# Attention backward for one query: half of V's gradient stored by GpSimd in pieces, in eight of 32 pairs

## Chip, cores and metric

One core of a Trainium2 chip. The metric is the device time of one execution in microseconds; lower is better. The core has the engines PE (TensorE), DVE (VectorE), ACT (ScalarE), POOL (GpSimd) and SP (SyncE), and sixteen DMA engines which all DMA queues share.

## What is computed

Attention of one query per head over 8192 keys, forward and backward, in bfloat16; 2 batches of 32 heads give 64 heads of 128 dimensions.

```python
B, H, Sq, Sk, D = 2, 32, 1, 8192, 128
def _fwd_reference(q, k, v):
    scale = q.shape[-1] ** -0.5
    scores = jnp.einsum("bhqd,bhkd->bhqk", q, k) * scale
    p = _softmax(scores, axis=-1)
    return jnp.einsum("bhqk,bhkd->bhqd", p, v)

_out, _vjp = jax.vjp(_f, q, k, v)
return (_out, *_vjp(grad_out))        # out, dq, dk, dv
```

K and V are read once (268 MB), their gradients written once (268 MB). For a single query the gradients of K and V are outer products: of the score gradients with q, and of the softmax weights with the output's gradient.

## The kernel before

**Tiles.** Heads go in 32 pairs. A pair's K, or V, is a buffer of 128 partitions by 128 tiles of 128 numbers: 4 MB, 32 KB in a partition; head 0 fills partitions 0 to 63, head 1 the others. The buffers stand in a ring of six (`ring`), three pairs of K and V. V's gradient is written over V in its own buffer and K's over K; then the buffer is stored and loaded again for the pair three further on (K of pair g+3 goes where V of pair g was, V where K was).

**Stages.** A pair goes through 16 stages `j` of its own, in which K (0 to 7) and V (8 to 15) are turned by TensorE, 16 tiles a stage (`transposes`, L119, copied out of PSUM by ACT at L126 and four times a pair by DVE at L124), and multiplied with the query or the output's gradient one stage later (`products`, L136). What is left of the pair runs in stages 16 to 24, beside stages 0 to 8 of the next pair. `manual_schedule` keeps the order in which the code issues things; each engine runs its list in that order.

**Gradients.** The softmax weights are there after stage 11. From stage 12 on, TensorE forms the weighted sums (`weighted_rows`, L247), and DVE writes V's gradient chunk by chunk (`outer`, L275, 16 tiles of 128 x 2048 numbers a chunk), by these tables:

```python
OUT_V = {12: (0,), 13: (1, 2), 14: (3,), 15: (4, 5), 16: (6,), 17: (7,)}
OUT_K = {19: (0, 1), 20: (2,), 21: (3, 4), 22: (5,), 23: (6, 7)}
STORE = {18: 0, 24: 1}
```

Between them DVE computes `deltas` (L218, in the next pair's stage 0) and `weights_k` (L231 to L241, in its stage 1), which K's gradient needs. TensorE's `sums` (L187) of the second kind needs `deltas`. In stage 24 `combine` (L264) ends the pair's part on TensorE.

**DMA.** SP's queue issues all loads (`load`, L108), ACT's all stores (`store`, L283). At stage 18 the whole of V's gradient is stored by one DMA of 4 MB, and the load of K for the pair three further on is put behind it; at stage 24 the same is done with K's gradient and V's load. A load waits for the store that empties its buffer. The last pair's gradients go out in quarters of 1 MB. Two small loads of 16 KB (`nat`) at the start bring q and the output's gradient, and two small stores at the end write the output and q's gradient. GpSimd sets up constants at the start (its two `wz` memsets at L295) and then does nothing.

Of the kernel before, what the change touches and what calls it, by code (L numbers as in the profile page):

```python
# [11 lines left out]
BF16 = mybir.dt.bfloat16  # L12
# [2 lines left out]
CH = 16  # L15
HC = CH // 2
RING = 6


@with_exitstack  # L20
def kernel(
# [11 lines left out]
    nc = tc.nc  # L33
    B, H, Sq, D = q.shape
    Sk = k.shape[2]
    P = nc.NUM_PARTITIONS
# [4 lines left out]
    NT = 2 * Sk // P  # L41
    NCH = NT // CH
# [5 lines left out]
    const = ctx.enter_context(tc.tile_pool(name="const", bufs=1))  # L48
# [18 lines left out]
    q_rows = q.rearrange("b h s d -> (b h s) d")  # L67
# [4 lines left out]
    def by_pairs(x):  # L72
        rows = x.rearrange("b h s d -> (b h s) d")
        return rows.rearrange("(g p n) d -> g p n d", p=P, n=NT)

    k_v, v_v, dk_v, dv_v = (by_pairs(x) for x in (k, v, out_2, out_3))
# [8 lines left out]

    ring = [kvp.tile([P, NT, D], BF16, name=f"ring{i}") for i in range(RING)]
    acc = ps_one.tile([P, 4 * D], F32, name="acc", tag="acc")
# [12 lines left out]
    pairs = [Pair() for _ in range(NP)]  # L100
# [6 lines left out]
    def load(g, w):  # L107
        nc.sync.dma_start(out=pairs[g].kv[w][:], in_=(k_v, v_v)[w][g])  # L108
# [4 lines left out]
    def transposes(g, j, u):  # L113
        x = pairs[g]
        w, c = divmod(j, NCH)
        tp = ps_tp.tile([P, HC, P], F32, name="tp", tag="tp")
        for i in range(HC):
            n = c * CH + u * HC + i
            nc.tensor.matmul(  # L119
                tp[:, i, :], lhsT=x.kv[w][:, n, :], rhs=ident_bf[:], start=True, stop=True  # L120
            )
        ev = evp.tile([P, HC, P], BF16, name="ev", tag="ev")
        if (j, u) in ((8, 0), (9, 0), (10, 0), (11, 0)):
            nc.vector.tensor_copy(out=ev[:], in_=tp[:])  # L124
        else:
            nc.scalar.copy(out=ev[:], in_=tp[:])  # L126
        x.ev[j, u] = ev

    def products(g, j, u):
        x = pairs[g]  # L130
        w, c = divmod(j, NCH)
        ev = x.ev.pop((j, u))
        cols = (qT_all, doT_all)[w][:, 2 * g : 2 * g + 2]
        for i in range(HC):
            n = c * CH + u * HC + i
            nc.tensor.matmul(  # L136
                scores(w)[:, :, n], lhsT=ev[:, i, :], rhs=cols, start=True, stop=True
            )

    def spread_row(g, w):  # L140
        pb = misc[:, (2 + w) * D : (3 + w) * D]
        for s, hs in enumerate(halves):
            nc.tensor.matmul(  # L143
                pb[hs],
                lhsT=ident_bf[0:BH, 2 * g + s : 2 * g + s + 1].to_broadcast([BH, HP]),
                rhs=nat[:, 1 - w, :],
                start=True,
                stop=True,
            )
        x = pairs[g]  # L150
        x.row = rowp.tile([P, D], BF16, name="row", tag="row")
        nc.scalar.copy(out=x.row[:], in_=pb)  # L152
# [6 lines left out]
    def all_max(x):  # L159
        mT = sm[0:1, 2 * NT : 2 * NT + P]  # L160
        nc.tensor.transpose(mT, x.mp[:], ident_f[:])
        x.gm = work.tile([1, 2], F32, name="gm", tag="gm")
        nc.vector.reduce_max(out=x.gm[:], in_=mT.rearrange("o (s p) -> o s p", s=2), axis=AX.X)
# [21 lines left out]
    def sums(x, w):  # L185
        x.lsum = (dp if w else sm)[:, 2 * NT + P + 8 : 2 * NT + P + 9]
        nc.tensor.matmul(x.lsum, lhsT=block[:], rhs=x.ld[:, w : w + 1], start=True, stop=True)  # L187
# [55 lines left out]
    def weighted_rows(x, w, c):  # L243
        rows = x.kv[1 - w]
        for g in range(4):
            n = c * CH + 4 * g
            nc.tensor.matmul(  # L247
                acc[32 * g : 32 * g + 16, :],
                lhsT=wz[w][:, n // 4, :],
                rhs=rows[:, n : n + 4, :].rearrange("p n d -> p (n d)"),  # L250
                start=(w == 0 and c == 0),
                stop=(w == 1 and c == NCH - 1),
                tile_position=(0, 32 * g),
            )
# [5 lines left out]
    def combine(g):  # L260
        x = pairs[g]
        c = misc[:, 0:4]
        for j in range(4):
            nc.tensor.matmul(  # L264
                c, lhsT=x.accsb[:, j * D : (j + 1) * D], rhs=pick[:, j],
                start=(j == 0), stop=(j == 3),
            )
        nc.vector.tensor_copy(  # L268
            out=colsT[:, :, 2 * g : 2 * g + 2], in_=c.rearrange("p (w s) -> p w s", w=2)
        )  # L270

    def outer(x, w, c):
        n = c * CH
        row = x.row[:].rearrange("p (d t) -> p d t", t=2)
        nc.vector.tensor_tensor(  # L275
            out=x.kv[1 - w][:, n : n + CH, :].rearrange("p n (d t) -> p n d t", t=2),
            in0=row.unsqueeze(1).to_broadcast([P, CH, D // 2, 2]),
            in1=x.w2[w][:, n : n + CH, :].unsqueeze(2).to_broadcast([P, CH, D // 2, 2]),
            op=ALU.mult,
        )  # L280

    def store(g, w, a=0, b=NT):
        nc.scalar.dma_start(  # L283
            out=(dv_v, dk_v)[w][g][:, a:b, :], in_=pairs[g].kv[1 - w][:, a:b, :]
        )

    def outer_and_store(g, w, c):
        outer(pairs[g], w, c)
        if g == NP - 1 and c % 2:
            store(g, w, (c - 1) * CH, (c + 1) * CH)  # L290

    for i, src in enumerate((q_rows, do_rows)):
        nc.scalar.dma_start(out=nat[:, i, :], in_=src)
    for t in wz:
# [12 lines left out]
    STORE = {18: 0, 24: 1}  # L307

    with tc.manual_schedule():
        for g in range(RING // 2):  # L310
            load(g, 0)
            load(g, 1)
        for h in range(NP + 1):
            y = pairs[h] if h < NP else None
            x = pairs[h - 1] if h else None
            for j in range(NS):
                at = [(z, zg, s) for z, zg, s in ((x, h - 1, j + NS), (y, h, j)) if z]
                for u in range(2):
                    if y:
                        transposes(h, j, u)  # L320
                    if y and j:
                        products(h, j - 1, u)
                    elif x and j == 0:
                        products(h - 1, NS - 1, u)
                    if u == 0:
                        if y and j == 8:
                            spread_row(h, 0)
                        if x and j == 2:
                            spread_row(h - 1, 1)
                        if x and j == 8:  # L330
                            combine(h - 1)
                    else:
                        if y and j == 9:
                            all_max(y)
                        if y and j == 10:
                            exps(y)
                        if y and j == 11:
                            sums(y, 0)
                        if x and j == 1:
                            sums(x, 1)  # L340
                    if u == 1:
                        for z, zg, s in at:
                            for w, when in ((0, ACC_V), (1, ACC_K)):
                                for c in when.get(s, ()):
                                    weighted_rows(z, w, c)
                if y and j == 8:
                    row_max(y)
                if y and j == 11:
                    weights_v(y)
                if x and j == 0:  # L350
                    deltas(x)
                if x and j == 1:
                    weights_k(x)
                for z, zg, s in at:
                    if s in STORE and zg < NP - 1:
                        store(zg, STORE[s])
                        if zg + 3 < NP:
                            load(zg + 3, STORE[s])
                    for w, when in ((0, OUT_V), (1, OUT_K)):
                        for c in when.get(s, ()):  # L360
                            outer_and_store(zg, w, c)
                if x and j == 6:
                    acc_to_sbuf(x)
        for w, dst in enumerate((o_rows, dq_rows)):
            tps = ps_tp.tile([BH, P], BF16, name="tps", tag="tp")
            nc.tensor.transpose(tps[:], colsT[:, w, :], ident_bf[:])
            rows = evp.tile([BH, D], BF16, name=f"rows{w}", tag="ev")
            nc.scalar.copy(out=rows[:], in_=tps[:])
            nc.scalar.dma_start(out=dst, in_=rows[:])


# [28 lines left out]
```

## Time and profile before

| | |
|---|---|
| times of three runs | 1300.5 us median (1298.71 to 1301.36) |
| profiled execution | 1301.66 us, of it 1299.9 us span |
| mean granted TensorE clock | 0.85 |
| busy: PE, DVE, ACT, POOL | 1093.5, 930.0, 906.3, 2.0 us |
| DMA | 539.64 MB, 415 GB/s over the span |
| DMA queues of SP and ACT | 48.8% and 49.0% of sixteen engines' span |
| instruction fetch (two queues) | 2.69 MB, 0.7% |
| chain that ended last | DMA 63%, PE 24%, ACT 7%, DVE 3% |
| a load of 4 MB, from issue to landing | 27.6 to 27.8 us (median) |
| a store of 4 MB | 45.9 us (median) |

The span goes from the first instruction to the last. "Issue to landing" counts from the issuing instruction to the last of sixteen marks, one from each DMA engine that has done its share; a wait for a DMA ends with the sixteenth. A transfer spreads over the partitions, so each engine has a fixed share of the rows. A line such as `A <- B` in the waits says that A sat idle until B was done. Queue letters (SPq, ACTq) are an engine's issuing side.

### The profile page before, as it was taken

Reading aid. Unit: us, or ns where it says so; the run is one execution under the profiler, and the core shown is the slowest. Engines: PE = TensorE matmul, PEld = TensorE weight load, DVE = VectorE, ACT = ScalarE, POOL = GpSimd, SP = SyncE. Lnnn points to the kernel's source line nnn. Section 1 sums busy time; section 2 is a strip of 40 time slices with the busy share of each in tenths; the row PEclk is TensorE's granted clock in tenths of the full one; section 3 lists DMA queues with packets and bytes.
Section 4 is the critical chain, followed back from the end, with each engine's and each line's share of the span. In section 5 each row is a group of like instructions: output and inputs, shape, how many; then the busy total and the mean of one; then the engine's idle time right before and its main releaser. Section 6 shows DMA issues by size and latency. Waiting matters only on the chain.

```text
span 1299.9 us, 42160 instructions
## 1 busy us (share of the span) xinstructions
PE 1093.5 (84%) x19044; PEld 936.6 (72%) x19044; DVE 930.0 (72%) x1355; ACT 906.3 (70%) x1091; POOL 2.0 (0%) x10
## 2 busy tenths in 40 slices
PE   4999899988888889888888887898888988889883
PEld 3777787776777778777677776677677877778771
DVE  0888788767867677767786676776677666776775
ACT  4887778767866678757686576876578666786761
POOL 0000000000000000000000000000000000000000
PEclk9999989889988788868898688988788777887876
DMA  9999999999999999999999999999999999999986
GB/s 404 417 425 424 429 427 432 427 430 430 429 429 427 427 426 420 427 430 403 426 429 427 429 400 429 432 423 423 414 393 420 416 405 410 410 421 419 404 348 268
DMA packets 19796, 539.64 MB, mean 415 GB/s; under 512 B 2464, under 2 KB 2464, under 8 KB 2464
## 3 DMA queue, kind: packets, MB, share of 16 engines
q10 hardware_dynamic: 10400, 268.51, 49.0%
q1 hardware_dynamic: 9216, 268.44, 48.8%
q8 instruction: 149, 2.44, 0.7%
q14 instruction: 31, 0.25, 0.0%
HBM read 268.47 MB, written 268.47 MB: 413 GB/s over the span
## 4 chain that ended last, share of the span: by engine, by line
DMA 63%; PE 24%; ACT 7%; DVE 3%; issue 2%; ACTq 0%; SPq 0%; DVEq 0%
DMA ring<-in_v_dram 43%; DMA out_dram<-ring 19%; PE tp L119 15%; ACT ev L126 5%; PE misc L264 3%; PE dp L136 2%; PE acc L247 1%; DVE ring L275 1%; DMA nat<-in_grad_out_dram 1%; PE sm L136 1%; DVE ev L124 1%; PE sm L167 1%; ACT E_f L176 1%; ACT row L152 1%; PE sm L187 0%
## 5 line engine op out<-in xcount | busy, mean ns | idle before, releaser
L126 ACT CAST ev<-tp 128x1024 bf16<-128x1024 f32 x896 | 865.4, 1020 | 287.0 <-PE tp L119 273.4
L119 PE MATMUL tp<-ident_bf,ring 128*128 128x128 bf16 x8192 | 721.9, 240 | 148.7 <-DMA ring<-in_v_dram 73.8
L119 PEld LDWEIGHTS <-ring 128*128 128x128 bf16 x8192 | 581.3, 108 | 286.7 <-issue 189.6
L136 PEld LDWEIGHTS <-ev 128*128 128x128 bf16 x8192 | 338.3, 100 | 7.3 <-issue 5.7
L275 DVE TENSOR_TENSOR ring<-row,dS 128x2048 bf16<-128x2048 bf16 x256 | 298.9, 1220 | 41.7 <-PE acc L247 39.9
L275 DVE TENSOR_TENSOR ring<-row,P 128x2048 bf16<-128x2048 bf16 x256 | 300.2, 1221 | 36.8 <-PE acc L247 35.8
L124 DVE CAST ev<-tp 128x1024 bf16<-128x1024 f32 x128 | 156.7, 1225 | 135.1 <-PE tp L119 131.6
L136 PE MATMUL dp<-doT_all,ev 128*128 128x2 bf16 x4096 | 185.7, 167 | 2.2 <-issue 1.4
L136 PE MATMUL sm<-qT_all,ev 128*128 128x2 bf16 x4096 | 178.9, 165 | 3.8 <-issue 3.7
L247 PE MATMUL acc<-ring,wz 128*16 128x512 bf16 x2048 | 167.8, 396 | 3.2 <-DVE wz L191 2.3
L152 ACT CAST row<-misc 128x128 bf16<-128x128 f32 x64 | 18.1, 282 | 81.5 <-PE misc L143 74.8
L264 PE MATMUL misc<-pick,accsb 128*128 128x4 f32 x256 | 52.0, 326 | 17.5 <-ACT row L152 11.2
L264 PEld LDWEIGHTS misc<-pick,accsb 128*128 128x128 f32 x256 | 49.2, 286 | 23.2 <-ACT row L152 16.0
L247 PEld LDWEIGHTS <-wz 128*16 128x16 bf16 x2048 | 31.2, 86 | 11.0 <-issue 2.7
L218 DVE CUSTOM_DVE_ANT_0 dSu<-E_f,dp 64x128 f32<-64x128 f32 x64 | 18.3, 285 | 28.5 <-PE dp L136 28.0
L157 DVE TENSOR_REDUCE mp<-sm 64x1 f32<-64x128 f32 x64 | 18.5, 289 | 21.9 <-PE sm L136 21.2
L268 DVE CAST colsT<-misc 128x4 bf16<-128x4 f32 x32 | 5.1, 161 | 31.8 <-PE misc L264 31.8
L176 ACT ACTIVATE E_f<-sm,negm 64x128 f32<-64x128 f32 x64 | 23.2, 363 | 1.7
L236 DVE SCALAR_TENSOR_TENSOR dSu<-dp,negdelta,E_f 64x128 f32<-64x128 f32 x64 | 22.4, 350 | 2.2
L258 DVE COPY accsb<-acc 128x512 f32<-128x512 f32 x32 | 22.1, 692 | 2.0 <-PE acc L247 1.0
L191 DVE TENSOR_SCALAR wz<-dSu,rl 64x128 bf16<-64x128 f32 x64 | 18.1, 283 | 2.1
L191 DVE TENSOR_SCALAR wz<-E_f,rl 64x128 bf16<-64x128 f32 x64 | 18.1, 283 | 1.7
(42 smaller groups left out, 197.6 us busy)
## 6 DMA issues: line engine op xcount, KB each, us to landing
out_dram<-ring ACTq DMA_DIRECT2D x62, 4096.0 KB, 45.9
ring<-in_k_dram SPq DMA_DIRECT2D x32, 4096.0 KB, 27.6
ring<-in_v_dram SPq DMA_DIRECT2D x32, 4096.0 KB, 27.8
out_dram<-ring ACTq DMA_DIRECT2D x8, 1024.0 KB, 11.3
out_dram<-rows ACTq DMA_DIRECT2D x2, 16.0 KB, 9.7
nat<-in_q_dram ACTq DMA_DIRECT2D x1, 16.0 KB, 11.0
nat<-in_grad_out_dram ACTq DMA_DIRECT2D x1, 16.0 KB, 15.4
```

The lines of the kernel that those rows point to most:

```text
L119: nc.tensor.matmul(tp[:, i, :], lhsT=x.kv[w][:, n, :], rhs=ident_bf[:], start=True, stop=True)
L124: nc.vector.tensor_copy(out=ev[:], in_=tp[:])
L126: nc.scalar.copy(out=ev[:], in_=tp[:])
L136: nc.tensor.matmul(scores(w)[:, :, n], lhsT=ev[:, i, :], rhs=cols, start=True, stop=True)
L152: nc.scalar.copy(out=x.row[:], in_=pb)
L176: nc.scalar.activation(out=x.E[hs], in_=scores(0)[hs, s, :], func=ACT.Exp, bias=negm[hs], scale=scale, accum_out=x.ld[hs, 0:1],)
L191: nc.vector.tensor_scalar(out=wz[w][hs, :, 8 * w + 4 * s : 8 * w + 4 * s + 4], in0=src[hs].rearrange("p (m j) -> p m j", j=4), scalar1=s1[ ...
L236: nc.vector.scalar_tensor_tensor(out=x.dSu[hs], in0=scores(1)[hs, s, :], scalar=negdelta[hs], in1=x.E[hs], op0=ALU.add, op1=ALU.mult,)
L247: nc.tensor.matmul(acc[32 * g : 32 * g + 16, :], lhsT=wz[w][:, n // 4, :], rhs=rows[:, n : n + 4, :].rearrange("p n d -> p (n d)"), start= ...
L258: nc.vector.tensor_copy(out=x.accsb[:], in_=acc[:])
L264: nc.tensor.matmul(c, lhsT=x.accsb[:, j * D : (j + 1) * D], rhs=pick[:, j], start=(j == 0), stop=(j == 3),)
L275: nc.vector.tensor_tensor(out=x.kv[1 - w][:, n : n + CH, :].rearrange("p n (d t) -> p n d t", t=2), in0=row.unsqueeze(1).to_broadcast([P, ...
```

## The change

In pairs 1, 5, 9, ..., 29 (`RELIEF`, eight of them) the first half of V's gradient (tiles 0 to 63, 16 KB in a partition, 2 MB) is no longer part of ACT's store. As soon as DVE's chunk 3 has been issued (stage 14), GpSimd stores it by 24 DMAs, each of some rows (partitions) four apart. The pieces are laid out so that each group of rows goes to the DMA engines that move it in a full store, except the rows 16 to 19 and 48 to 51, the fifth engine's: these go out in four pieces of two rows (`fifth`) by way of eight other engines. For this the change counts on a place that goes round the sixteen engines with every GpSimd DMA, and moves that place on by small loads of 3 to 14 rows of 8 bytes from q into a spare tile (`turn`), eleven in an event, one at the start and one at the end. ACT's store at stage 18 sends the second half alone. K's load three pairs on now waits for both.

```diff
+RELIEF = range(1, 32, 4)
...
+    spare = const.tile([P // 8, 48], BF16)
+    turns = []
+
+    def turn(n):
+        i = 4 * (len(turns) % 12)
+        turns.append(n)
+        two = lambda t: t.rearrange("p (a b) -> p a b", a=2)
+        nc.gpsimd.dma_start(out=two(spare[0:n, i : i + 4]), in_=two(q_rows[0:n, 0:4]))
+
+    def store_by_fifteen(g):
+        dst, src = (t[:, 0 : NT // 2, :] for t in (dv_v[g], pairs[g].kv[1]))
+
+        def rows(lo, n, step=4, size=8192):
+            own = slice(lo, lo + step * (n - 1) + 1, step)
+            nc.gpsimd.dma_start(out=dst[own], in_=src[own], max_dma_last_dim=size)
+
+        def fifth(r):
+            rows(16 + r, 2, step=32)
+
+        for r in range(4):
+            if r == 1:
+                fifth(r)
+                turn(14)
+            rows(52 + r, 11)
+            rows(r, 4, size=16384)
+            if r == 0:
+                fifth(r)
+                turn(3)
+            elif r == 3:
+                turn(10)
+                fifth(r)
+                turn(9)
+            else:
+                turn(5)
+            rows(20 + r, 3)
+            if r == 2:
+                fifth(r)
+                turn(14)
+            rows(96 + r, 8)
+            rows(32 + r, 4, size=16384)
+            turn(5)
...
     def outer_and_store(g, w, c):
         outer(pairs[g], w, c)
+        if g in RELIEF and w == 0 and c == NCH // 2 - 1:
+            store_by_fifteen(g)
         if g == NP - 1 and c % 2:
             store(g, w, (c - 1) * CH, (c + 1) * CH)
...
+    turn(5)
     for i, src in enumerate((q_rows, do_rows)):
         nc.scalar.dma_start(out=nat[:, i, :], in_=src)
...
-                        store(zg, STORE[s])
+                        store(zg, STORE[s], NT // 2 if zg in RELIEF and not STORE[s] else 0)
...
             nc.scalar.dma_start(out=dst, in_=rows[:])
+        turn(11)
```

Every piece of 8 KB or 16 KB in a row is a packet or two on its engine; a full row of before is one packet of 32 KB. GpSimd's DMAs report to eight semaphores in turn, so each waits for the one eight before it.

## The prediction

> **What bounds the kernel now.** I read the page's slices first, then the windows by stage, the waits of SP's queue, the chain, and last DVE's timeline around the place of the edit.
>
> The slices say that the DMA engines never rest before the last 50 us, and that their rate falls late in the run:
>
> ```profile
> DMA  9999999999999999999999999999999999999986
> GB/s 404 417 425 424 429 427 432 427 430 430 429 429 427 427 426 420 427 430 403 426 429 427 429 400 429 432 423 423 414 393 420 416 405 410 410 421 419 404 348 268
> ```
>
> The windows put numbers on it (time, busy time of PE, PEld, DVE, ACT and POOL, then granted clock, DMA share, GB/s):
>
> ```profile
> 206.00:241.00 35.00, 31.45 (x595) 26.72 (x595) 29.24 (x43) 28.42 (x35) 0.00 (x0) 0.95 1.00 429
> 120.00:560.00 440.00, 379.95 (x6789) 325.28 (x6788) 332.25 (x479) 323.86 (x389) 0.00 (x0) 0.88 1.00 427
> 960.00:1240.00 280.00, 245.10 (x4073) 212.11 (x4071) 199.16 (x291) 194.49 (x234) 0.00 (x0) 0.80 1.00 413
> 1292.00:1298.00 6.00, 0.00 (x0) 0.00 (x0) 0.00 (x0) 0.00 (x0) 0.00 (x0) 0.50 0.06 26
> ```
>
> Share 0.06 is one engine of sixteen: one engine works alone for the last 6 us. It is slower all along. In the trace's packet records a 32 KB packet takes 1.213 us on most engines, and on one chain of back-to-back packets (330 to 362 us) mostly 1.22 to 1.34 us. The landing marks of the stores show it too: its mark trails the last but one by 2.3 us at 231 us, 14 at 574, 25 at 979, and then no more, since the others have run out of stores to work ahead on. From there the kernel goes at this engine's pace, 413 GB/s for 427. So what the change is after is there.
>
> SP's waits and the chain say how loads hang on stores, and how fast the compute engines are when data is there:
>
> ```profile
> SPq L108 <- DMA out_dram<-ring: 1174.6, 58, 50.7
> ```
>
> ```profile
> 65.70 1.06 PE misc L264 x8
> ...
> 206.31 1.05 PE misc L264 x8
> ...
> 241.07 1.06 PE misc L264 x8
> ...
> 251.53 27.80 DMA ring<-in_v_dram
> 280.71 1.87 PE misc L264 x8
> ...
> 1252.73 1.26 PE misc L264 x8
> ```
>
> `combine` (L264) runs once a pair. Up to 241 us no load is in the chain and a pair takes (241.07 - 65.70)/5 = 35.1 us; after that V's load closes each pair, at (1252.73 - 241.07)/25 = 40.5 us. So compute has 5.4 us to spare in a pair, 21 us in four.
>
> **The wait that the change adds.** This decides my forecast. The order of the changed program's instructions on DVE, with their waits, has in each of the eight pairs:
>
> ```
> TensorTensor ring<-row,P 128x2048 [waits PE]      (chunk 3)
> TensorTensor ring<-row,P 128x2048 [waits DMASW4,DMASW3,DMASW5,DMASW2,DMASW6,DMASW1,DMASW7,DMASW0,PE]      (chunk 4)
> ```
>
> The pieces read tiles 0 to 63 of the ring buffer, chunk 4 writes tiles 64 to 79, so no data forces this; but the pieces take every fourth partition, and the wait is in the program. Its counts are those of the last data piece of the event, the 34th of 35 GpSimd DMAs (24 of data, 11 `turn`). So DVE stops after chunk 3 until GpSimd's whole half of V's gradient has landed. Where that is, in a pair of before:
>
> ```profile
> 294.89 6.90 DVE L275 TENSOR_TENSOR ring<-row,P 128x2048 bf16<-128x2048 bf16 x6 [1.23 <-PE acc L247]
> 302.39 0.28 DVE L218 CUSTOM_DVE_ANT_0 dSu<-E_f,dp 64x128 f32<-64x128 f32 x1 [0.60 <-PE dp L136]
> ```
>
> Six multiplies run back to back; the gap would open at about 299.5, behind the fourth. Behind the waiting multiply stand chunks 5 to 7, `deltas` (L218), `weights_k` and all of K's gradient. PE and ACT get two stages further (about 5 us), to `sums` of K, which needs `deltas`; then PE stands too, and after the wait DVE first makes up that work. So I count the whole wait T as lost to compute.
>
> **T.** No GpSimd DMA is in the trace of before, so it is bounded by neighbours.
> - From below: a DMA's issue takes 0.34 us on ACT's queue (L283, min 338 ns). 34 x 0.34 = 11.6 us, and some 4 us for the last to land (the last 1,024 KB store, issued at 1287.84, is marked by fifteen engines by 1291.8): T = 15.
> - From above: the two small loads at the start, beside one loaded queue:
>
> ```profile
> nat<-in_q_dram ACTq DMA_DIRECT2D x1, 16.0 KB, 11.0
> nat<-in_grad_out_dram ACTq DMA_DIRECT2D x1, 16.0 KB, 15.4
> ```
>
> In the packet records their five packets on an engine each wait for a 1.213 us packet of the other queue, turn about; the second landed 4.97 us after the first. 34 x 4.97 = 169 us if the queues stayed loaded. They don't: with DVE standing no new store comes and no load follows. In the first event both queues run dry in some 50 us (the outstanding stores' landing time, up to 50.7 us above). Later ones find less: after a stall DMA has caught up, then gains 39.2 us of work a pair (16.8 MB at 428 GB/s) against 35.1 us of compute, 16 us in four pairs, and the transfers then under way add some 10. So about 25 us with loaded queues.
> - My value: an engine gets some 55 packets in an event (16 to 18 of data, 34 completion marks, some dummies), 1.6 a piece. While queues are loaded, a turn is 1.2 us (one queue) to 2.4 us (two): 1.9 to 3.9 us a piece, 6 to 13 pieces in 25 us. The other 21 to 28 go at GpSimd's issue price, between 0.34 us and about 1 us: 7 to 28 us. T = 32 to 53; I take 40, the middle.
>
> The Trainium skill (DMA: Bandwidth & Descriptors, Latency and other measured facts) gives about 1 us to the first byte of a GpSimd DMA against 0.6 us for one of SP or ACT. If that were paid once a piece, 34 us would be issue alone and T about 45; no run here shows it yet.
>
> **The other parts.**
> - Relief: 8 events x 8 rows x 16 KB come off the slow engine, 64 x 0.61 us = 39 us, and eight others get 4.9 us each. If DMA still set the pace this would bring back the late rate, 280 us x (1 - 413/427) = 9.2 us; the slow engine's lag on the last V load, 7.0 us (its marks, 1244.3 and 1251.3); the lag at the end, 6.8 us (1291.8 to 1298.5); less 4.9. That is 18 us.
> - ACT's eight V stores shrink to 2,048 KB: same count, nothing on ACT.
> - K's load three pairs on (L108) waits for the pieces as well, with V's load behind it on SP. It leaves some 53 us after the event before (352.6 against 299.5), so a T of 40 is covered; DVE's wait comes first.
> - GpSimd is busy 2.0 us in all, so its issues delay nobody but through their landing. `turn(5)` at the start precedes the `wz` memsets, not needed before chunk 0's products 25 us later; `turn(11)` is off the path.
>
> **The sum.** With data ahead, as after every stall, compute sets the pace. Thirty-first `combine` at 65.70 + 30 x 35.1 = 1118; from it to the end 1299.9 - 1252.7 = 47.2, less the 6.8 us lag: 40.4. Span without waits 1158, and 1.8 around it (1301.66 against 1299.9): 1160. Eight waits of 40: 1160 + 320 = 1480 us. The profiled execution lies 1.2 us above the median of the runs, which is nothing beside T's spread. The time stays above before as long as T exceeds (1301.7 - 1160)/8 = 17.7 us.
>
> **Rivals.**
> - *The pieces land in under 17 us*, so that the spare 21 us of four pairs swallow the wait, and relief does what it is for: 1301.7 - 18 = 1283 us, faster. For it: 15 us is the floor above, and with idle queues a DMA lands in 4 us. Against it: at that T the DMA engines stay saturated, and then a turn costs 1.2 to 2.4 us and 34 completion marks alone need 41 us. 0.11; another 0.01 for a T that just balances.
> - *The pieces go one after another*, each leaving when the one before has landed: between 1.6 us (the 4.0 us of the last 1,024 KB store, less 8 packets of 0.31) and 2.4 us (a turn beside two loaded queues) a piece, 54 to 82 us; at 2.1, T = 72 and 1160 + 8 x 72 = 1736 us. The spacing of the two small loads, 4.97 us, speaks for it; eight semaphores, which let eight pieces be under way, speak against it. 0.08. The Trainium skill (DMA: Bandwidth & Descriptors, Rules for kernel authors) speaks against such pieces too: a transfer under 64 KB pays mostly overhead. Its fit for a GpSimd DMA (same page, Anatomy of one DMA) has 2.0 us fixed in each, by which 34 in series would take an estimated 73 us.
> - *The pieces miss the slow engine's place* (which engine a GpSimd DMA uses is nowhere in this trace): then relief is nothing or hits another engine. Under my forecast DMA has time to spare and this moves little; it is in the 0.80 that is left.
>
> **How the numbers follow.** Likeliest case, T about 40, chance 0.80, its own range 1360 (T 25) to 1620 (T 57): 1480. The range reaches down to T = 21, 1328, and up to T = 65, 1680; it leaves out the faster rival and the serial one. 0.2%, 2.6 us, is about what a measurement of this kernel can tell from none: faster 0.11, same 0.01, slower 0.88.
>
> **What would show it.** In the profile after: DVE L275 with eight idle stretches of some 40 us, put down to a DMA out of ring; PE and ACT idle in the same stretches and busy shares some 12% lower; DMA slices with dips to 7 or 8 at eight places; pairs between events at 35 to 36 us with no load in the chain; no engine alone at the end. Wrong would be: L275 waits under 18 us (the first rival), waits over 60 (the second), or a pace of 40 us between events, which would mean that DMA still binds.

## The result and the profile after

The changed kernel takes 1529.9 us, the median of four runs (1524.9 to 1533.7), against 1300.2 for the kernel before; the ratio is 1.1765, 95% interval 1.1725 to 1.1806. It is slower by 230 us. The forecast of 1480 lies 50 us below that, and its range of 1328 to 1680 holds it. In the changed kernel the lines have moved by one: `outer` is L276, `combine` L265, `deltas` L219, `sums` L188, `transposes` L120, `load` L109; the pieces are L299, the turns L292.

The slices of the profile after (span 1522.8 us) show the eight events:

```profile
DVE  1816886077860877607776187751888328872387
POOL 0040001300013000130001300013000130001300
...
DMA  9976999769996799956999679995999958999458
GB/s 407 421 327 268 372 406 426 307 275 377 413 427 279 290 413 413 427 230 278 409 408 427 250 306 422 411 426 206 356 421 430 412 208 331 430 425 406 180 223 333
```

Wherever POOL shows a 3 or 4, DVE falls to 0 to 3 and the DMA rate to 180 to 327 GB/s. Before, the DMA row was nines up to its last two slices. The table of waits names the place (time in all, times, longest):

```profile
DVE ring L276 <- DMA spare<-in_q_dram: 337.5, 8, 44.9
...
PE dp L188 <- DVE ld L219: 322.7, 9, 43.2
POOL out_dram L299 <- DMA out_dram<-ring: 108.8, 26, 8.8
```

DVE's multiply waits eight times, 42.2 us each, and TensorE behind it at `sums` for `deltas`. One event in the timeline (start, busy time, engine, operation; what it waited for in brackets):

```profile
255.60 4.63 DVE L276 TENSOR_TENSOR ring<-row,P 128x2048 bf16<-128x2048 bf16 x4 [0.58 <-PE acc L248]
...
260.52 1.72 POOL L299 DMA_DIRECT2D out_dram<-ring  x3 [143.73 <-DVE ring L276]
...
273.82 0.58 POOL L299 DMA_DIRECT2D out_dram<-ring  x1 [8.83 <-DMA out_dram<-ring]
...
293.29 0.54 POOL L292 DMA_DIRECT2D spare<-in_q_dram  x1 [3.21 <-DMA out_dram<-ring]
293.82 1.13 POOL L299 DMA_DIRECT2D out_dram<-ring  x2
...
303.22 0.55 POOL L292 DMA_DIRECT2D spare<-in_q_dram  x1
305.14 2.36 DVE L276 TENSOR_TENSOR ring<-row,P 128x2048 bf16<-128x2048 bf16 x2 [44.91 <-DMA spare<-in_q_dram]
...
308.07 0.58 PE L188 MATMUL dp<-ld,block 128*128 128x1 f32 x2 [43.17 <-DVE ld L219]
```

Four chunks, then 44.91 us of nothing. GpSimd's first eight DMAs leave by 265.0; each further one waits for the one eight before it, so by 293.3 only 17 of 35 are out, and nine have landed. Then the queues of SP and ACT have run dry, and the other 18 leave in 10.0 us, 0.55 us each. The windows below are cut just ahead of each `combine` (time, busy time of PE, PEld, DVE, ACT, POOL, granted clock, DMA share, GB/s): the pair of this event, the first and the third behind it, then the first and the second behind the next event:

```profile
243.30:322.40 79.10, 33.98 (x595) 28.91 (x595) 28.76 (x43) 28.41 (x35) 19.41 (x35) 0.68 0.74 306
322.40:360.00 37.60, 34.84 (x595) 29.83 (x595) 28.88 (x43) 28.34 (x35) 0.00 (x0) 0.82 0.88 353
...
397.20:432.30 35.10, 31.54 (x595) 26.71 (x595) 29.21 (x43) 28.67 (x36) 0.00 (x0) 0.95 1.00 426
...
510.00:544.80 34.80, 31.43 (x596) 26.72 (x596) 29.10 (x43) 28.20 (x35) 0.00 (x0) 0.95 0.93 373
544.80:583.10 38.30, 35.10 (x599) 29.95 (x599) 29.30 (x44) 29.14 (x35) 0.00 (x0) 0.82 1.00 410
```

The event's pair takes 79.1 us, the three behind it 37.6, 37.2 and 35.1. TensorE has the same matmuls in each.

### The profile page after: what moved, and what is told of

It is laid out like the page before. It is cut to its first block, busy times and chain, and to the rows that moved or that the text cites. A ratio compares the mean times of both kernels' runs of the same rounds, so it can differ in the third digit from the quotient of the medians.

```text
span 1522.8 us, 42521 instructions
## 1 busy us (share of the span) xinstructions
PE 1072.6 (70%) x19044; PEld 915.1 (60%) x19044; DVE 924.6 (61%) x1355; ACT 907.4 (60%) x1091; POOL 158.4 (10%) x292
## 3 DMA queue, kind: packets, MB, share of 16 engines
q0 software_dynamic: 11072, 16.82, 3.0%
## 4 chain that ended last, share of the span: by engine, by line
PE 45%; DMA 17%; ACT 15%; DVE 11%; POOL 5%; issue 5%; ACTq 1%; DVEq 0%; POOLq 0%
PE tp L120 28%; DMA out_dram<-ring 14%; ACT ev L127 14%; PE acc L248 6%; DVE ring L276 6%; POOL out_dram L299 4%; PE dp L137 3%; PE sm L137 3%; DMA spare<-in_q_dram 2%; PE misc L265 2%; POOL spare L292 1%; DVE ev L125 1%; DVE dSu L237 1%; DMA nat<-in_grad_out_dram 1%; DVE wz L192 1%
## 5 line engine op out<-in xcount | busy, mean ns | idle before, releaser
L120 PE MATMUL tp<-ident_bf,ring 128*128 128x128 bf16 x8192 | 717.2, 238 | 79.9 <-ACT ev L127 61.4
L120 PEld LDWEIGHTS <-ring 128*128 128x128 bf16 x8192 | 576.5, 108 | 218.8 <-issue 204.8
L276 DVE TENSOR_TENSOR ring<-row,P 128x2048 bf16<-128x2048 bf16 x256 | 300.7, 1220 | 372.1 <-DMA spare<-in_q_dram 337.5
L276 DVE TENSOR_TENSOR ring<-row,dS 128x2048 bf16<-128x2048 bf16 x256 | 298.4, 1219 | 42.1 <-PE acc L248 31.9
L188 PE MATMUL dp<-ld,block 128*128 128x1 f32 x64 | 13.4, 278 | 322.7 <-DVE ld L219 322.7
L299 POOL DMA_DIRECT2D out_dram<-ring x192 | 109.4, 575 | 1221.3 <-DVE ring L276 1100.7
L188 PEld LDWEIGHTS dp<-ld,block 128*128 128x128 f32 x64 | 11.2, 219 | 323.7 <-DVE ld L219 323.7
L292 POOL DMA_DIRECT2D spare<-in_q_dram x90 | 48.0, 533 | 48.8 <-DMA out_dram<-ring 43.3
L265 PE MATMUL misc<-pick,accsb 128*128 128x4 f32 x256 | 35.7, 263 | 17.5 <-ACT row L153 11.2
L265 PEld LDWEIGHTS misc<-pick,accsb 128*128 128x128 f32 x256 | 32.9, 201 | 22.7 <-ACT row L153 15.4
L248 PEld LDWEIGHTS <-wz 128*16 128x16 bf16 x2048 | 31.2, 86 | 10.9 <-issue 2.8
L219 DVE CUSTOM_DVE_ANT_0 dSu<-E_f,dp 64x128 f32<-64x128 f32 x64 | 18.2, 284 | 20.0 <-PE dp L137 19.6
```

Of the source, the lines that this page charges most:

```text
L120: nc.tensor.matmul(tp[:, i, :], lhsT=x.kv[w][:, n, :], rhs=ident_bf[:], start=True, stop=True)
L248: nc.tensor.matmul(acc[32 * g : 32 * g + 16, :], lhsT=wz[w][:, n // 4, :], rhs=rows[:, n : n + 4, :].rearrange("p n d -> p (n d)"), start= ...
L265: nc.tensor.matmul(c, lhsT=x.accsb[:, j * D : (j + 1) * D], rhs=pick[:, j], start=(j == 0), stop=(j == 3),)
L276: nc.vector.tensor_tensor(out=x.kv[1 - w][:, n : n + CH, :].rearrange("p n (d t) -> p n d t", t=2), in0=row.unsqueeze(1).to_broadcast([P, ...
L292: nc.gpsimd.dma_start(out=two(spare[0:n, i : i + 4]), in_=two(q_rows[0:n, 0:4]))
L299: nc.gpsimd.dma_start(out=dst[own], in_=src[own], max_dma_last_dim=size)
```

## The experiments

The theory: the false wait of DVE costs the time, and its length comes from the many packets and marks of GpSimd's DMAs beside loaded queues. The rivals: another wait on the pieces stands behind the first (K's load three pairs on), or the path through GpSimd is slow as such, by its bytes. In the diffs, the changed kernel is the minus side unless said otherwise. "Landing" is the time from the first to the last data packet of an event's pieces, from the trace's packet records, as a median over events; it is 37.7 us in the changed kernel.

### Is the split or GpSimd's path dear by itself?

The same half store by ACT at the same place, without GpSimd:

```diff
-            store_by_fifteen(g)
+            store(g, 0, 0, NT // 2)
```

> No GpSimd DMA at all: the first half of V's gradient goes out by ACT's queue at the place of the pieces, the second at stage 18. Theory W: no wait on DVE, no relief: 1295 to 1305 us, as before. Rival Q: the same. A time over 1310 would say that splitting the store, or sending half of it earlier, costs by itself.

Measured: 1301.5 us, ratio 0.9996 (0.9981 to 1.0012). An eighth of the stores in halves costs nothing.

The same half in one GpSimd DMA of 128 rows, without turns:

```diff
-        def rows(lo, n, step=4, size=8192):
...
-        for r in range(4):
...
+        nc.gpsimd.dma_start(out=dst, in_=src)
```

> The half of V's gradient goes out by GpSimd at the same place as one DMA of 128 rows of 16 KB; no turns, no engine passed by, and no wait on DVE's chunk 4 in the program. Theory N (the pieces are slow because there are 35 DMAs, each with its issue and its completion mark waiting a turn on every engine): about 9 packets an engine instead of 55, landed in some 22 us, long before K's load needs it: 1297 to 1305 us, and the slow engine's lag grows to 25 us or more as before. Rival G (whatever GpSimd stores beside two loaded queues is slow): K's load is late, over 1320 us.

Measured: 1308.9 us (ten times, from 1300.0 to 1315.8), ratio 1.0047 (1.0014 to 1.008). Its issues:

```profile
out_dram<-ring POOLq DMA_DIRECT2D x8, 2048.0 KB, 28.7
```

The same 2 MB by the same queue lands 28.7 us after the issue (22.3 by packets). The path through GpSimd is at most 0.8% of the time; it is the pieces that cost. One engine still works alone at the end, as before (DMA share 0.06 from 1291.5 to 1297.5 us).

### The false wait, taken out in two ways

The pieces after V's last chunk, so that no chunk waits for them:

```diff
-        if g in RELIEF and w == 0 and c == NCH // 2 - 1:
+        if g in RELIEF and w == 0 and c == NCH - 1:
```

> The same pieces, but issued after V's last chunk (stage 17), so that no chunk of V's gradient stands behind them on DVE. Theory W (DVE's wait for the pieces is the whole loss): the idle time of some 42 us an event is gone, DVE's chunk multiplies wait no more than before, and the time is between 1280 and 1305 us. Rival Q (the pieces themselves are the loss, since beside two loaded queues they take 80 us or more and K's load three pairs on waits for them): SP's waits grow, PE waits for K, and the time stays above 1350 us.

Measured: 1365.7 us, 1.049 (1.0472 to 1.0508).

Pieces of neighbouring partitions, same number, sizes and place; then chunk 4's wait is not in the program:

```diff
-            own = slice(lo, lo + step * (n - 1) + 1, step)
+            own = slice(lo, lo + n)
...
-            rows(52 + r, 11)
+            rows(52 + 11 * r, 11)
```

(and so on for the other groups)

> The same number of pieces, rows, turns and place (stage 14), but each piece takes neighbouring partitions instead of every fourth; in the program DVE's chunk 4 then no longer waits for GpSimd's DMAs. Theory W: 1275 to 1300 us, 225 us or more under the changed kernel, with the pieces landing beside DVE's work. Rival Q: the pieces hold K's load, above 1350 us. If the fifth engine is passed by as meant, its lag on the stores stays under 10 us; if not, it grows to 25 us as before.

Measured: 1399.0 us, 1.0753 (1.0728 to 1.0777). So 164 and 131 of the 230 us come back with DVE's wait, and the rest does not. In both, `DVE ring <- DMA spare` is gone from the waits and this stands there instead, first of the late, then of the neighbouring pieces:

```profile
PE tp L120 <- DMA ring<-in_k_dram: 138.5, 7, 26.0
```

```profile
PE tp L120 <- DMA ring<-in_k_dram: 166.4, 7, 28.4
```

This is the load of K three pairs on, which waits for the pieces that empty its buffer, 20 and 24 us late in each of the seven events that have such a load. Landing is 72.6 and 84.3 us here: DVE no longer stands, so new stores keep coming and the queues of SP and ACT stay loaded for longer, in most events 58 to 62 us (late pieces) and 71 to 74 us (neighbouring), counted from the pieces' first packet until loads and stores keep fewer than four engines busy. Both theories were half right: the first wait is most of the loss, and the second is behind it. The pairs with such a wait take 58 to 68 us (the first of each run 45 and 52), the others 34 to 41, most of them under the 40.5 of before; these win back part of the waits.

### What makes T

Without the eleven turns in an event (24 DMAs instead of 35):

```diff
     def store_by_fifteen(g):
+        turn = lambda n: None
```

> The eight events keep their 24 data pieces but lose the eleven turns (8-byte loads). Packets per number of DMAs decide (my theory: each DMA costs GpSimd an issue of 0.56 us, and on every engine a turn for its data packets and for its 4-byte marks as long as the queues are loaded): in the changed kernel the wait was 42.2 us with 35 DMAs; the first 25 us or so, in which the queues are loaded, stay about as they are, and of what follows eleven issues at 0.56 to 0.8 us go, 6 to 9 us a time. Wait at DVE L276 (L277 here) 33 to 36 us, time 1530 - 8 x 7 = about 1474 (1460 to 1490). Rival (the 2 MB, or the wait for the loaded queues to run dry, set the wait, and not the number of DMAs): wait 42, time 1520 to 1530.

Measured: 1484.5 us, 1.1407 (1.1353 to 1.1461). The wait stands in two rows here (lines one further on for the pieces):

```profile
DVE ring L276 <- DMA out_dram<-ring: 256.0, 7, 43.1
DVE ring L276 <- DMA spare<-in_q_dram: 40.4, 1, 40.4
```

That is 296.4 / 8 = 37.1 us for 42.2: 5.1 us for eleven tiny DMAs, about what eleven issues of 0.55 us cost, and 41 of the 45 us that the time fell by. The wait is somewhat over the 33 to 36 expected, the time within its bounds; the rival (no change) is out.

Every row's 16 KB in one packet:

```diff
-        def rows(lo, n, step=4, size=8192):
+        def rows(lo, n, step=4, size=16384):
```

> Same 35 DMAs in the same place, but every row's 16 KB goes in one packet where most went in two of 8 KB: 8 or so data packets on an engine and event for 14 to 16; marks and turns as before. If only the number of packets counted, 6 of 86 fewer: wait 42 down to 39 us, time 1505 (1490 to 1520). If the number of DMAs counts (issue, and the wait for the landing of the DMA eight back), 42 and 1520 to 1530. The two are close; the run says how far the packet size matters at all, which bears on the wide 16 KB pieces of other runs.

Measured: 1533.5 us, 1.1766 (1.1713 to 1.182); wait 41.5 us. GpSimd's queue carries 9,024 packets for 11,072, and T stays within 1 us. (The pieces also fall on other engines here; see the last run of the next section.)

Half as many events, pairs 1, 9, 17, 25:

```diff
-RELIEF = range(1, 32, 4)
+RELIEF = range(1, 32, 8)
```

> The changed kernel with four events instead of eight (pairs 1, 9, 17, 25). Theory W with spare compute time: eight pairs lie between events, whose spare time of 5.4 us a pair (43 us) takes in one wait of 42 us nearly whole, so DMA nearly sets the pace: 1300 to 1350 us, well under the middle. Rival L (each event costs its 42 us less the same 21 us, or simply a fixed share): the middle between before and after, 1415 us.

Measured: 1405.3 us, 1.0804 (1.0787 to 1.082), above every number expected. The row says why:

```profile
DVE ring L276 <- DMA spare<-in_q_dram: 196.8, 4, 56.4
```

T is 49.2 us, not 42.2. With seven pairs between events (three in the changed kernel) the pieces meet loaded queues for longer: in the last three events the last packet of a load ends 37 to 42 us behind the first of the pieces, in the last seven of the changed kernel 24 to 29. 1160 + 4 x 49.2 is 1357, and the pairs in between, 36.6 us for 35.1, add most of the rest. T is no constant of the pieces: it goes with what is queued.

### What makes the landing long: bytes or number

Everything halved in size and nothing in number: a quarter of V by the same 35 DMAs, on the kernel with neighbouring partitions, which is the minus side here:

```diff
-        dst, src = (t[:, 0 : NT // 2, :] for t in (dv_v[g], pairs[g].kv[1]))
+        dst, src = (t[:, 0 : NT // 4, :] for t in (dv_v[g], pairs[g].kv[1]))
...
-        def rows(lo, n, size=8192):
+        def rows(lo, n, size=4096):
```

(likewise 16384 to 8192 twice, and ACT's store begins at `NT // 4`)

> The kernel with pieces of neighbouring partitions, with everything halved in size but nothing in number: a quarter of V (1 MB) goes out by the same 24 pieces and eleven turns at the same place, 8 KB of a row (two packets of 4 KB, or one of 8 KB for the two groups that had one of 16), and ACT stores the other three quarters at stage 18. With the full pieces the landing took 84 us an event and the time was 1399. If the number of packets and DMAs sets the landing (each waits its turn beside loaded queues, whatever its size): 75 to 84 us, K's load late by 15 to 24 us in seven events, time 1370 to 1400. If the bytes set it: 42 to 50 us, K's load hardly late, time 1300 to 1330.

Measured: 1373.2 us, 1.053 (1.0472 to 1.0587). The GpSimd queue of the two kernels, neighbouring pieces first (packets, MB, share of sixteen engines):

```profile
q0 software_dynamic: 11072, 16.82, 5.6%
```

```profile
q0 software_dynamic: 11072, 8.43, 2.8%
```

Half the bytes, the same 11,072 packets, and the same landing: 84.4 us for 84.3. The bytes don't set it. On an engine that is 11,072 / (8 x 16) = 86 packets in an event, most of them marks or loads of 4 or 8 bytes that take 9 ns. The packet records show how they wait: on back-to-back chains load, store and GpSimd packet take turns, and a mark of 9 ns stands behind packets of 1.213 us of the other two queues.

The landing is not 86 times one price, though. Two windows (columns as above) of an event of the neighbouring pieces, whose data packets go from 592.0 to 675.4 us:

```profile
592.00:640.00 48.00, 42.61 (x750) 35.94 (x749) 36.43 (x53) 36.23 (x45) 4.46 (x8) 0.86 1.01 421
...
664.00:676.00 12.00, 1.07 (x20) 0.75 (x19) 1.81 (x2) 1.83 (x2) 6.53 (x12) 0.63 0.48 72
```

SP issues a load of K at 588.8 us, one of V at 609.8 and none before 676.1, since the next load of K waits for the pieces. So the other queues run dry at some 663.5 us. By then 23 of the 35 DMAs have left; the other 12 leave in 9 us. In the quarter kernel 13 are left at that point. So the number of turns decides that an event isn't through before the queues run dry, and that moment sets most of the 84 us in both kernels: it comes 71 to 74 us behind the first packet here, and 72 to 76 us in most events of the quarter kernel. K's load is still late, 16 us a time:

```profile
PE tp L120 <- DMA ring<-in_k_dram: 128.8, 8, 24.3
```

The pieces of neighbouring partitions without turns and in packets of 16 KB (the kernel of neighbouring pieces is the minus side again):

```diff
+        turn = lambda n: None
...
-        def rows(lo, n, size=8192):
+        def rows(lo, n, size=16384):
```

> The pieces of neighbouring partitions (no false wait of DVE) without the eleven turns and with 16 KB packets: per engine and event 8 data packets and some 24 to 45 small ones, where the kernel with turns and 8 KB packets had 14 and 72 (86 packets, 83 to 94 us from the first to the last beside loaded queues, time 1399). Theory that each packet, marks too, costs its turn beside loaded queues: landing falls to 86 x (32 to 53)/86 = 32 to 53 us, K's load three pairs on is hardly late any more (in the kernel with turns 24 us each of seven times), and the time is 1300 to 1335. Rival (GpSimd's DMAs beside loaded queues are slow by their bytes or by GpSimd's own handling): landing over 75 us, time 1380 to 1400.

Measured: 1403.8 us, 1.0789 (1.0721 to 1.0856), landing 84.9: the expectation missed. Only 24 DMAs and 6,208 packets go by GpSimd's queue, 48 an engine on average, but they are no longer dealt evenly. In one event (591 to 678 us) one chain of back-to-back packets holds 24 data packets where an even share is 8, and it ends with the landing; several others hold none. The missing turns aren't needed for that: in the run above with all turns and packets of 16 KB, three chains at the end of one event (683.96 to 686.15 us) hold a packet each of the last pieces of three, eight and four rows, back to back. In the changed kernel, with two packets of 8 KB in each of the eight rows, the last pieces of eight and four rows move at the same time, on engines of their own (303.5 to 304.5 us). So the crowding goes with the packets of 16 KB. Here too the other queues run dry, some 75 us into an event. The run leaves open what fewer packets, evenly dealt, would save.

### Fewer pieces, and which engine is passed by

Two pieces of 8 and 120 neighbouring rows and three turns, in place of the 35 DMAs:

```diff
+        rows(120, 8)
+        turn(8)
+        rows(0, 120)
+        turn(9)
+        turn(8)
```

> The relief with few DMAs: the half goes out as 8 rows and 120 rows, two packets of 8 KB a row, with three turns, so that the 120 rows use fifteen engines from the sixth on and pass by the fifth; five GpSimd DMAs an event instead of 35. Theory N: some 25 packets an engine, landed within 60 us of stage 14, K's load late by under 8 us, and the relief works: 1275 to 1300 us, with a lag under 10 us at the end. Rival G: over 1320 us.

Measured: 1312.8 us, 1.0089 (1.0068 to 1.011). The landing is 47.7 us, within the 53 us that K's load leaves, and TensorE's weight loads wait 13.5 us for K in the whole run. The same with the first `turn(5)` made `turn(10)` and the last made `turn(6)`, so that another engine should be passed by:

> e6_few with the place moved on by ten instead of five at the start, so that the tenth engine is passed by and not the fifth. If the fifth engine is the slow one and the place goes round as the change counts on: same waits as e6_few, but the lag grows to 25 us and the time is 10 to 25 us over e6_few. If the engines are not chosen that way, or another one is slow, both kernels give the same time within 4 us.

Measured: 1311.1 us, 1.0071 (1.005 to 1.0092), the same within the intervals. In both no engine works alone at the end. The window from 8 to 2 us before the end of the first of them:

```profile
1300.40:1306.40 6.00, 2.26 (x10) 1.97 (x10) 2.49 (x4) 0.52 (x2) 0.00 (x0) 0.50 0.97 396
```

The DMA share is 0.97, where before it was 0.06. Yet the pairs still take some 40 to 41 us. The chain of the slow engine (1.24 to 1.27 us a packet) carries 16 to 18 of GpSimd's data packets in an event, and the chain with only two of them runs at the normal 1.213. That speaks against the slow engine being the one passed by. The records don't name engines, so it is not proved. Where the 10 to 12 us over before come from stays open.

Last, whole V by the same five DMAs at stage 18, instead of ACT's store, in four pairs (the call behind chunk 3 is gone):

```diff
-RELIEF = range(1, 32, 4)
+RELIEF = range(3, 31, 8)
...
+                        if zg in RELIEF and not STORE[s]:
+                            store_by_fifteen(zg, 0, NT, 16384)
```

> The same five DMAs, but in four pairs (3, 11, 19, 27), for the whole of V's gradient, at stage 18 in place of ACT's store, with packets of 16 KB: the same 4 x 8 x 32 KB off the fifth engine. Theory N: as few packets per byte as can be, 1275 to 1295 us, the fastest of this call if the relief works. Rival G: over 1320 us.

Measured: 1329.8 us, 1.0222 (1.0173 to 1.0271). The large piece lands 61.6 us after its issue, and TensorE waits 31.2 us for K, where it waited 5.2 before (for V 59.9, before 73.8). No version here beats the kernel before; the nearest is the plain split, which equals it.

## Why the prediction was right, and where it was off

**The added wait.** Right: eight waits at L276 behind chunk 3, on the last data pieces by way of their eight semaphores, with PE and ACT idle within 5 us. That it is the larger part of the loss is shown twice over by the kernels without it.

**T.** 42.2 us measured for 40. The form was right, a stretch beside loaded queues and a rest at GpSimd's issue price, but its sizes were off, and the errors partly cancel. In the event shown the queues stay loaded for 33 us, not 25, with nine pieces landed, within the 6 to 13; the other 18 leave at 0.55 us, within the 0.34 to 1 taken, in 10 us where the prediction had 7 to 28. An engine got 86 packets in an event, not 55: 67 of them have 4 bytes, where 34 marks and some dummies were counted. And the middle of 32 to 53 is 42.5, not 40. So it is in part luck that T came within 2.2 us. The issue price itself:

```profile
L299 POOL DMA_DIRECT2D out_dram<-ring x192: 532/587/607, 81.2 to 1427.6; - x192
```

So GpSimd spends some 19 us of T on issuing. The Trainium skill (DMA: Bandwidth & Descriptors, Latency and other measured facts) has about 1 us to the first byte by this path. Once the queues are dry, pieces leave every 0.55 us here, so that 1 us is not paid once a piece, one after another.

**Compute's pace.** 35.1 us a pair was the step that failed most. The 22 pairs between events take 796.1 us, 36.2 each. 35.1 came from a stretch with a granted clock of 0.95. Pairs with a mean clock of 0.95 take 34.5 to 35.1 us here as well, those at 0.82 take 37.4 to 38.5 (rows above), and the 22 lie between 0.82 and 0.95. The place behind a stall doesn't tell which: the first pair behind the eight events had 0.82, 0.82, 0.95, 0.86, 0.95, 0.90, 0.95 and 0.90. What sets the clock was not tried.

**The sum.** Against the profiled execution of 1524.9 us, 45 us were missing: 337.5 - 320 = 17.5 for T, 22 x 1.1 = 24 for the pace, and some 2 for the events' own pairs, which take 77.6 us, 35.4 without the wait. The 39.7 us from the 31st `combine` to the end are as forecast (40.4).

**The cover for K's load.** "A T of 40 is covered" holds in the changed kernel, where no load of K is in the larger waits. It holds only because DVE stands: the landing is 72 to 85 us once it doesn't, more than the 53 us of cover (which late pieces have less of). The prediction named this wait and then left it out of the cases; with DVE's wait gone, it is the second loss: 64 and 98 us over before in the two kernels that take out DVE's wait alone.

**The relief.** No engine is alone at the end, as forecast: from 8 to 2 us before the end the DMA share is 0.94. But stalls give a slow engine time to catch up, so that says nothing on relief. Where the DMA sets the pace (two pieces, above) the lag at the end is gone too, and the time is still 0.7 to 0.9% over before. The 18 us were not found.

**The rivals.** T under 17 is out. Pieces in series (T 72, 1736 us) are out for T: the longest wait is 44.9 us, and up to eight are under way at once. The rule of the Trainium skill beside it (DMA: Bandwidth & Descriptors, Rules for kernel authors) is that a transfer under 64 KB pays mostly overhead. The same landing of 84 us for half the bytes agrees, though the largest pieces, of 176 and 88 KB, are above that size.

## What to carry to other kernels

Before splitting a transfer over a software queue, count the turns that its packets and completion marks must wait beside the other queues, not its bytes: a turn stood behind one or two packets of 1.213 us here, and 2 MB that land in 22 us as one DMA took 72 to 85 us in 24 pieces. Read the changed program's waits for false ones, since slices with a step can tie an instruction to a DMA of other tiles; and when such a wait is taken away, price the next wait with the queues full. A pace measured in an undisturbed stretch is not the pace between stalls.

## What had not been expected of the hardware

- A mark of 4 bytes, 9 ns by itself, takes a turn of its own behind packets of 1.213 us: halving all sizes left the landing at 84 us.
- The granted clock of a pair between events lies between 0.82 and 0.95, with the same matmuls, and no rule by the stall in front of it is seen (0.82 right behind two of them, 0.95 behind three).
- Pieces whose rows are one packet of 16 KB each crowd on the same engines, with the turns or without: one chain got 24 data packets in an event and others none. With two packets of 8 KB in a row, a piece of eight rows and the next of four ran side by side.
- Four stalls with longer spaces cost 49.2 us each where eight cost 42.2.
